# Lightning attention in windows of 256 tokens, on four 64x64 tensor tiles at a time, ahead of an MLP

## The chip, the cores and the metric

The kernel runs on one core of one Trainium2 chip. The metric is the device time of one execution in microseconds (us); less is better. "The span" is the length of the execution that was profiled, which is about 1.7 us shorter than the timed figure of the same execution. Executions carry a state, fast or slow; only fast ones are compared below, unless a sentence says otherwise. A time given alone is the median of all executions of a kernel.

In the views, PE is the engine of matmuls and PEld its weight loads; DVE, ACT and POOL are the vector, scalar and GpSimd engines, SP issues most transfers; PSUM is the memory that PE writes to.

## The reference, cut to what matters

Four batches, eight heads, 768 tokens, head dimension 64. Attention is linear, with a decay `lam` per head, so it runs along the tokens with a 64 x 64 state per head and batch. Its output goes through a mean-centred, scaled MLP of 512 to 2048 to 512 with a residual.

```python
for b in range(nb):                                   # nb blocks along the tokens
    qb, kb, vb = (q[:, :, sl], k[:, :, sl], v[:, :, sl])
    intra = np.einsum('bhic,bhjc->bhij', qb, kb) * Dmask[None]
    intra = np.einsum('bhij,bhjd->bhid', intra, vb)
    inter = np.einsum('bhid,bhde->bhie', qb * lam_pow[None], kv_state)
    out[:, :, sl] = intra + inter
    # ... kv_state = lam_block * kv_state + (decayed k)^T v
# x = out as [batch, token, 512]
xn = (x - mu) / np.sqrt(var + 1e-06) * g_ln
ch = np.maximum(xn @ w_ch1, 0.0) @ w_ch2
return (x + ch).astype(np.float32)
```

## The kernel before

It goes through 24 chunks of 128 tokens, batch after batch. Tokens lie on the 128 partitions, so a load moves 256 B per token and head (64 numbers of 4 B). Attention of a chunk is in steps: casting and scaling (`in_k`, `in_q`, `in_v`), transposes (`p1`), scores and mask, the next state, and the output with the mean and the centred copy (`p3`); `p4` transposes that copy for the MLP. The first projection is `m1`, the second `m2`.

```python
def load_tile(t, after_pool=False):
    b, c = divmod(t, nb)
    # ...
    for name, src in (("k", k), ("q", q), ("v", v)):
        f = inp.tile([128, H, D], F32, tag=name + "in", name=name + "in")
        # ... with after_pool, a POOL write to f delays the load
        nc.sync.dma_start(f, src[b, :, c * C:(c + 1) * C, :].rearrange("h p d -> p h d"))

def scores(t):
    # ...
    for p in range(NP):                # NP = 4 pairs of heads
        for e in range(2):             # two row tiles, 64 rows by 128 columns
            half = slice(e * D, (e + 1) * D)
            nc.tensor.matmul(sc[e][:, p, :], lhsT=s["kT"][half, p, :], rhs=s["qT"][half, p, :], ...)

def next_state(t):
    # ...
    for p in range(NP):                # full array; two of the four 64x64 blocks are not used
        nc.tensor.matmul(pk[:, p, :], lhsT=s["kb"][:, 2 * p:2 * p + 2, :], rhs=s["vb"][:, 2 * p:2 * p + 2, :], ...)

def p3(t):
    # ...
    for h in range(H):
        nc.tensor.matmul(po[:, h, :], lhsT=s["mA"][:, h % 2, h // 2, :], rhs=s["vb"][:, h, :], ...)
    if inter:
        for p in range(NP):
            nc.tensor.matmul(po[:, 2 * p:2 * p + 2, :], lhsT=s["qT"][:, p, :], rhs=s["S"][:, p, :], ...)

# the start, weights and loads only
load_tile(0); load_tile(1); ...; load_tile(2); load_tile(3)
# ... chunk 0 and chunk 1 ...
in_k(2, nc.scalar); in_q(2); load_w1(0); in_v(2)
# ...
in_k(3, nc.scalar); in_q(3); in_v(3); load_w1(1)
# ...
load_w1(2); load_w1(3)
# ... then load_w2(0..3), load_tile(5..7), and MLP groups 0 and 1
```

After the start, a plan of MLP units (one unit is 4 `m2` matmuls, or `m1` work of about the same length, some 0.9 us) has the attention steps put in between by hand.

## Time and profile before

| | before |
|---|---|
| median of the first 3 runs, us | 228.71 (227.81 to 229.04) |
| span, us | 226.0 |
| PE busy | 206.9 us, 92% |
| `m2` starts at, us | 43.9 |
| matmuls | 1736 |

The prediction below shows the page, the chain and the windows. The list of waits of PE before the change (the columns: who waited, for whom, us in total, times, longest):

```profile
PE tk L161 <- DVE kb L141: 5.7, 1, 5.7
PE sc L185 <- ACT qT L172: 2.8, 4, 0.8
...
PE pm L279 <- DMA w<-in_moe_w_ch_dram: 1.6, 1, 1.6
```

The long waits all belong to the start; 5.7 us is the wait for the very first data. No input load stands in the list. The list of DMA issues (how many, KB each, median us from issue to landing):

```profile
vin<-in_v_dram SPq DMA_DIRECT2D x24, 256.0 KB, 4.9
...
w<-in_moe_w_ch_dram POOLq DMA_DIRECT2D x8, 512.0 KB, 8.3
```

### The profile page before, as it was taken

How to read it: one execution, taken by the hardware profiler on the slowest of the kernel's cores; microseconds unless marked ns; L12 is line 12 of the kernel's file. 1: busy time of each engine (PE TensorE's matmuls, PEld its weight loads, DVE VectorE, ACT ScalarE, POOL GpSimd, SP SyncE). 2: the span in 40 equal slices, each digit the busy share in tenths (PEclk: the TensorE clock that was granted, in tenths of full speed). 3: DMA queues.
4: the chain of work that ended last, by engine and by line, in shares of the span. 5: the costliest groups of instructions: out<-in, count | busy, mean ns of one | idle time of the engine just before them, and what ended most of it. 6: DMA issues, size and time to landing. Idle time of an engine off the chain costs nothing.

```text
span 226.0 us, 4339 instructions
## 1 busy us (share of the span) xinstructions
PE 206.9 (92%) x1736; PEld 131.4 (58%) x1736; DVE 104.5 (46%) x202; ACT 95.5 (42%) x191; POOL 88.0 (39%) x103
## 2 busy tenths in 40 slices
PE   0567969999999899999999999999999999999992
PEld 0346848844677587577587466545654565455540
DVE  2467610054457556766754474267428345420021
ACT  5655645611256255146146067404750375127400
POOL 2559518025670948874156638301562020000000
PEclk9999988999999999999999999999999999999999
DMA  5998992999999999999999999939432511040012
GB/s 117 225 228 134 184 211 36 187 191 230 209 290 225 234 239 209 188 226 191 219 200 263 228 219 198 220 100 217 109 70 70 142 25 23 33 131 2 0 67 72
DMA packets 107555, 35.93 MB, mean 159 GB/s; under 512 B 100112, under 2 KB 104464, under 8 KB 107536
## 3 DMA queue, kind: packets, MB, share of 16 engines
q1 hardware_dynamic: 103168, 31.47, 68.8%
q0 software_dynamic: 4224, 4.19, 11.7%
q8 instruction: 13, 0.21, 0.4%
q14 instruction: 6, 0.05, 0.1%
q10 hardware_dynamic: 144, 0.00, 0.0%
HBM read 27.53 MB, written 6.29 MB: 150 GB/s over the span
## 4 chain that ended last, share of the span: by engine, by line
PE 81%; DMA 6%; DVE 4%; SPq 3%; ACT 2%; issue 1%; POOL 1%; DVEq 0%
PE pm L292 36%; PE pm L279 35%; DMA w<-in_moe_w_ch_dram 4%; PE sc L185 3%; SPq L65 3%; DMA qin<-in_q_dram 2%; PE po L224 2%; PE po L228 2%; PE pk L198 1%; DVE stats L233 1%; ACT x L231 1%; DVE xc L237 1%; PE tq L169 1%; DVE Stmp L205 1%; PE xt L255 1%
## 5 line engine op out<-in xcount | busy, mean ns | idle before, releaser
L279 PE MATMUL pm<-xT,w 128*128 128x256 bf16 (+2 forms) x704 | 92.2, 287 | 1.6 <-DMA w<-in_moe_w_ch_dram 1.6
L292 PE MATMUL pm<-w,hT 128*128 128x512 bf16 x384 | 88.2, 379 | 0.0
L282 ACT ACTIVATE hT<-pm 128x384 bf16<-128x384 f32 (+1 forms) x112 | 60.0, 536 | 57.9 <-PE pm L279 57.2
L279 PEld LDWEIGHTS <-w 128*128 128x128 bf16 x704 | 63.6, 100 | 23.9 <-DMA w<-in_moe_w_ch_dram 1.8
L292 PEld LDWEIGHTS <-hT 128*128 128x128 bf16 x384 | 36.2, 98 | 39.2
L206 POOL TENSOR_TENSOR Sn<-Stmp,lamC 128x512 bf16<-128x512 f32 x16 | 20.3, 1271 | 65.4 <-DVE Stmp L205 65.3
L233 DVE BATCH_NORM_STATS2 stats<-x 128x6 f32<-128x512 f32 x24 | 16.7, 694 | 44.4 <-ACT x L231 44.3
L303 DVE SCALAR_TENSOR_TENSOR o<-pm,rstd,x 128x512 f32<-128x512 f32 (+1 forms) x25 | 18.0, 725 | 32.1 <-PE pm L292 31.9
L188 DVE TENSOR_TENSOR mA<-sc,tril 128x512 bf16<-128x512 f32 x48 | 30.7, 682 | 2.8 <-PE sc L185 2.8
L231 ACT COPY x<-po 128x512 f32<-128x512 f32 x24 | 14.0, 584 | 34.9 <-PE po L228 22.7
L149 POOL TENSOR_TENSOR vb<-vin,lam_v 128x512 bf16<-128x512 f32 x24 | 25.1, 1044 | 2.4 <-PE po L224 2.0
L237 DVE SCALAR_TENSOR_TENSOR xc<-po,mv,g_row 128x512 bf16<-128x512 f32 x24 | 18.0, 751 | 2.3
L145 POOL TENSOR_TENSOR kq<-qin,lam_q 128x512 bf16<-128x512 f32 x15 | 15.7, 1044 | 1.2 <-DMA qin<-in_q_dram 1.2
L145 POOL TENSOR_TENSOR qb<-qin,lam_q 128x512 bf16<-128x512 f32 x9 | 9.4, 1042 | 15.3 <-DMA qin<-in_q_dram 14.7
L205 DVE TENSOR_TENSOR Stmp<-pk,Sn 128x512 f32<-128x512 f32 x16 | 10.9, 683 | 4.2 <-PE pk L198 4.1
L224 PEld LDWEIGHTS <-mA 128*128 128x128 bf16 x192 | 9.2, 102 | 3.9 <-DVE mA L188 0.4
L161 PE MATMUL tk<-ident,kb 128*128 128x128 bf16 x36 | 4.4, 259 | 6.8 <-DVE kb L141 5.7
L224 PE MATMUL po<-vb,mA 128*128 128x64 bf16 x192 | 10.4, 199 | 0.1
L141 POOL CAST kq<-kin 128x512 bf16<-128x512 f32 x15 | 9.2, 611 | 2.0 <-DMA kin<-in_k_dram 2.0
L258 ACT ACTIVATE std<-mv,eps_t 128x1 f32<-128x1 f32 x24 | 7.0, 293 | 5.4 <-DVE mv L235 5.4
L163 ACT COPY kT<-tk 128x512 bf16<-128x512 bf16 x9 | 5.2, 581 | 7.9 <-PE tk L161 7.9
L260 DVE RECIPROCAL rstd<-std 128x1 f32<-128x1 f32 x24 | 3.8, 158 | 10.2 <-ACT std L258 10.0
(51 smaller groups left out, 97.3 us busy)
## 6 DMA issues: line engine op xcount, KB each, us to landing
kin<-in_k_dram SPq DMA_DIRECT2D x24, 256.0 KB, 4.5
qin<-in_q_dram SPq DMA_DIRECT2D x24, 256.0 KB, 4.6
vin<-in_v_dram SPq DMA_DIRECT2D x24, 256.0 KB, 4.9
out_dram<-o SPq DMA_DIRECT2D x23, 256.0 KB, 2.9
w<-in_moe_w_ch_dram POOLq DMA_DIRECT2D x8, 512.0 KB, 8.3
g_row<-in_moe_g_ln_dram SPq DMA_DIRECT2D x1, 256.0 KB, 4.6
xT<-xc SPq DMA_TRANSPOSE x16, 3.5
out_dram<-o SPq DMA_DIRECT2D x2, 128.0 KB, 1.8
```

Of the source, the lines that this page charges most:

```text
L145: nc.gpsimd.tensor_tensor(st[t]["qb"], qkv_in[t]["q"], lam_q[:, :, None].to_broadcast([128, H, D]), op=ALU.mult)
L149: nc.gpsimd.tensor_tensor(vb, qkv_in.pop(t)["v"], lam_v[:, :, None].to_broadcast([128, H, D]), op=ALU.mult)
L188: nc.vector.tensor_tensor(mA[:, e], sc[e], tril[:, None, :].to_broadcast([128, NP, 128]), op=ALU.mult)
L206: s["pool"] = lambda: nc.gpsimd.tensor_tensor(Sn, tmp, lamC, op=ALU.mult)
L224: nc.tensor.matmul(po[:, h, :], lhsT=s["mA"][:, h % 2, h // 2, :], rhs=s["vb"][:, h, :], start=(h == 0), stop=(not inter and h == H - 1), ...
L231: nc.scalar.copy(x, po.rearrange("p h d -> p (h d)"))
L233: nc.vector.bn_stats(stats, x)
L237: nc.vector.scalar_tensor_tensor(xc, in0=po.rearrange("p h d -> p (h d)"), scalar=mv[:, 0:1], in1=g_row, op0=ALU.subtract, op1=ALU.mult)
L279: nc.tensor.matmul(pm[:, b, :], lhsT=w1[n // W2K][:, kk, (n % W2K) * 128:(n % W2K + 1) * 128], rhs=xT_of[g][:, kk, 0:N], start=(b == 0 and ...
L282: nc.scalar.activation(hT[:, u * NB:(u + 1) * NB, 0:N], pm, ACT.Relu)
L292: nc.tensor.matmul(acc[i], lhsT=hT[:, kk, i * 128:(i + 1) * 128], rhs=w2[kk // W2K][:, kk % W2K, :], start=(kk == 0), stop=(kk == KB - 1))
L303: nc.vector.scalar_tensor_tensor(o[:, sl], in0=a[:, sl], scalar=rstd, in1=x[:, sl], op0=ALU.mult, op1=ALU.add)
```

## The change

Two chunks of one batch are taken together as a window of 256 tokens; the four batches take turns, so a window's state is needed only four windows later. Chunk a lies on partitions 0 to 63 and chunk b on 64 to 127, two neighbouring tokens on each partition. So a load moves 512 B at once, and each attention matmul uses a 64 x 64 quarter of the PE array, with four different quarters next to each other in the program. No block of a matmul is wasted any more. The price is more matmuls (2848), a row order that the store has to undo (two stores with strided rows), and a short DVE read of the output (`reader`) between the two halves of the state matmuls. The order of the start and the plan are new too.

```diff
-    def load_tile(t, after_pool=False):
-        b, c = divmod(t, nb)
... (cut)
-            nc.sync.dma_start(f, src[b, :, c * C:(c + 1) * C, :].rearrange("h p d -> p h d"))
+    def source(src, u, hs):
+        cc, b = divmod(u, B)
+        return src[b, hs, cc * W:(cc + 1) * W, :].rearrange("h (p j) d -> p h (j d)", j=2)
... (cut)
+    def scores(u, hf, early=False):
... (cut)
+        for i in range(2):
+            for jk in range(2):
+                for ab in range(2):
+                    for e in range(2):
+                        nc.tensor.matmul(sc[e][half[ab], i, jk, :], lhsT=kT[half[e], 2 * hf + i, jk, half[ab]],
+                                         rhs=qT[half[e], 2 * hf + i, :, half[ab]],
... (cut; kv and inter are tiled in the same way)
+    def av(u, pairs, chunks=(0, 1)):
... (cut)
+        for p in pairs:
             for e in range(2):
... (cut)
+                for j in range(2):
+                    for jq in range(2):
+                        for ab in chunks:
+                            nc.tensor.matmul(s["po"][ab][half[jq], 2 * p + e, :],
+                                             lhsT=s[f"mA{p // 2}"][half[ab], e, p % 2, j, half[jq]],
+                                             rhs=s["vb"][half[ab], 2 * p + e, j],
... (cut)
+    def reader(u):
+        s = st[u]
+        for ab in range(2):
+            if s["S"][ab] is not None:
+                seen = wk.tile([128, H], F32, tag="seen", name="seen")
+                nc.vector.tensor_copy(seen, s["po"][ab][:, :, 0])
... (cut)
-    sizes = [2, 2, 1, 1, 2, 2, 2, 3, 3, 3, 3]
+                    nc.sync.dma_start(rows[j][:, ab, sl], o[half[j], ab, sl])
... (cut)
+    sizes = [2, 2, 2, 2, 2, 2, 4, 4, 4]
... (cut; the start, weights and loads only)
+    load_w1(0)
+    load_window(1, after_pool=True)
... (cut)
+    load_w1(1)
+    load_w1(2)
... (cut)
+    in_q(1, nc.gpsimd)
+    in_v(1, nc.gpsimd)
+    load_w1(3)
+    load_window(2, after_pool=True)
+    load_w2(0)
... (cut; the steady part: what is sent ahead of window u)
+    def ahead_of(u):
+
+        for f, w in ((transpose_dma, u + 1), (load_window, u + 3), (p0, u + 2)):
+            if w < NU:
+                f(w)
```

`p0` is the casting and scaling of one window's k, q and v, most of it on POOL. `kv` is the product for the next state, `av` scores times v, `inter` q times state. Tiles in the views: `kq` and `vb` scaled k, q and v; `kqT` the transpose of `kq`; `sc` scores, `mA` the same masked; `pk` state product, `Stmp` its sum with the old state, `Sn` the decayed new state; `po` output, `xc` its centred copy, `xT` the transpose of that; `pm` a product of the MLP.

## The prediction

Its sum: 226.0 - 2.4 - 2.2 - 5.6 - 0.8 = 215.0 us of span, 217.5 us timed. The -2.4 is the choice of 17.6 us for attention, between the cases of 15.6 and 31.2 that stand there.

> **What bounds the kernel now.** I read the page first: the busy line and the forty slices.
>
> ```profile
> span 226.0 us, 4339 instructions
> PE 206.9 (92%) x1736; PEld 131.4 (58%) x1736; DVE 104.5 (46%) x202; ACT 95.5 (42%) x191; POOL 88.0 (39%) x103
> ...
> PE   0567969999999899999999999999999999999992
> ...
> PEclk9999988999999999999999999999999999999999
> DMA  5998992999999999999999999939432511040012
> ```
>
> PE is full from slice 7 (about 40 us) to the end; no other engine passes half. DMA is also full for two thirds of the span, so the second question is whether PE ever waits for it. The chain that ended last, in order of time, answers:
>
> ```profile
> 8.90 5.43 DMA qin<-in_q_dram
> ...
> 22.71 8.51 DMA w<-in_moe_w_ch_dram
> 31.27 10.57 PE pm L279 x80
> 42.29 1.75 PE pm L279 x16
> 44.04 0.86 PE pm L292 x4
> 45.13 0.33 PE sc L185 x8
> ...
> 95.37 0.23 PE po L224 x8
> 95.61 0.22 PE po L228 x4
> ```
>
> Up to 31 us the chain is transfers and a latency chain. From there it is PE, almost without a break: MLP work with small attention pieces between. The first projection's weights land at 31.27, the second projection (L292) starts at 44.04. The table of windows confirms the two stages (columns: stretch, length, then busy time and instructions of PE, PEld, DVE, ACT, POOL, clock, DMA share, GB/s):
>
> ```profile
> 0.00:10.00 10.00, 2.33 (x22) 1.70 (x23) 2.40 (x9) 5.91 (x10) 3.31 (x11) 1.00 0.86 161
> 20.00:30.00 10.00, 8.35 (x86) 6.81 (x83) 6.79 (x14) 6.33 (x14) 5.43 (x7) 1.00 0.98 154
> 30.00:40.00 10.00, 8.73 (x65) 7.21 (x66) 0.17 (x1) 4.68 (x9) 5.69 (x8) 0.83 0.66 112
> 100.00:120.00 20.00, 20.00 (x193) 14.55 (x192) 12.05 (x25) 9.09 (x18) 8.15 (x9) 1.00 1.28 216
> ```
>
> Busy PE is not useful PE, so I took the start-to-start distances of single matmuls in the trace: 216 ns for 512 columns, 56 for 128, 29 for 64 (columns divided by 2.4 plus 2.5 ns). Charging each matmul that much gives **192.3 us of work**. The other 33.7 us of the span: 5.7 before the first matmul, 13.2 in stops over 130 ns (11.6 of them before 31 us), 10.3 in small delays (cold clock before 40 us, and switches below), 4.5 after the last matmul. At 44.04 us, 20.9 us of work is done, so 23 us are lost by then.
>
> [...] the 8 score matmuls (64 rows) start in pairs 3 ns apart, a pair each 56 ns. Four tiles do not occur before. [...] 152 ns from the last full-array matmul to the first score one, 149 ns back, in place of 56, so about 95 ns a switch. [...] In the packet records a 256 B packet takes a median 18 ns, a 2048 B packet 84: a line through both gives 8.6 ns plus 1 ns per 27 B, so I estimate 27.5 ns at 512 B. [...]
>
> **Part by part.**
>
> *MLP matmuls.* Group sizes go from [2,2,1,1,2,2,2,3,3,3,3] to six of 2 and three of 4. m1 before: 320 x 109 + 256 x 162.5 + 128 x 56 = 83.7 us; after: 352 x 109 + 64 x 56 + 192 x 216 = 83.5. m2 stays 384 x 216 = 82.9. No gain.
>
> *Attention matmuls, before.* 192 scores as 96 pairs x 56 = 5.4; 192 po x 29 = 5.6; 80 pk and 80 state matmuls x 56 = 9.0. Sum 20.0 us. Transposes: 104 x 56 = 5.8. With the MLP this is 192.4, which matches the 192.3 counted.
>
> *Attention matmuls, after.* Scores 12 windows x 32 = 384 of 128 columns. Of 64 columns: kv 8 x 32 + 4 x 16 = 320, av 768, inter 8 x 32 + 4 x 16 = 320, so 1408. The loops put four different tiles next to each other. If four run together: 96 quads x 56 = 5.4, 352 quads x 29 = 10.2, sum **15.6 us (-4.4)**. [...] If only two run together: 192 x 56 + 704 x 29 = 31.2 (+11). I choose 17.6 us (-2.4), near the first, because row pairs already behave ideally.
>
> *Transposes.* 48 for k and q (was 72), 16 for the MLP input (was 32): 64 x 56 = 3.6, **-2.2 us**.
>
> *Mode switches.* Before, two per chunk: 24 x 2 x 95 ns = 4.6 us. After, a window's attention runs in two blocks (two switches each): 12 x 4 x 95 ns, the same.
>
> *Loads.* 18.9 MB as 256 B packets: 73728 x 18 / 16 = 83 us of all DMA engines; after, 36864 x 27.5 / 16 = 63, so 20 us of DMA time freed. After 44 us PE waits for no load, so there this is hidden. In the start it counts. Before the m1 weights, the old kernel moves four tiles (3.1 MB) and has issued the first weight load only at 15.4 us; the new one issues it once the first half of k is seen (about 5 us) and loads one window (1.6 MB) ahead of it. My count: window 0 in 5.3 us of DMA, gain vector 0.7, window 1 5.3, four m1 weight chunks at 3.1 each (2 KB read per packet of 96 ns): 23.7 us, plus 2.6 us until the first packet. POOL issues the last m1 chunk only after window 1's v has been scaled (about 20 us), so I put its landing at 27 to 29 us against 31.3. After that about 10.5 us of PE work (the last quarter of group 0, group 1, window 2's scores) precede m2, which then starts at about **39 us instead of 44**. By then 21.5 us of work is done, so 17.5 us are lost instead of 23.1: **-5.6 us**.
>
> *Vector side.* States are 64 x 64 blocks now: 16 DVE sums of 683 ns become 256 elements, an estimated 415 ns, and 16 POOL decays of 1271 about half. Masks stay 48 x 682. Fence reads add 20 x about 0.15 us. All beside PE: worth nothing directly, but with the k, q tiles transposed by DMA earlier I expect the two DVE-bound breaks at 69 to 78 us (1.3 us of stops) to shrink: -0.8.
>
> *Tail.* The last output half, its store and 4.5 us stay.
>
> **Sum.** 226.0 - 2.4 - 2.2 - 5.6 - 0.8 = 215.0 us of span. The timed median is 2.7 us above the traced span, so **217.5 us**, 5% faster.
>
> **Rivals.** (a) *PE becomes issue- or weight-load-bound.* PE instructions rise from 1736 matmuls to about 1856 + 992 = 2848, and a block holds 128 of them. No stretch of the trace before shows PE fed faster than a pair of instructions per 28 ns for longer than 8 matmuls. If only bursts overlap, attention costs 11 us more on the bound engine, and the start's gain is eaten: 226 to 230. For it: no evidence of sustained feeding[...]. Against: the pairs at 3 ns. (b) *The start does not move.* It may stay a chain of load, cast, transpose, copy, scores, mask, av, norm; a whole window of 256 tokens goes through it at once, and window 1 shares the DMA with the weights. Then m2 starts at 44 again and only PE work is saved: 223. For it: in slice 2 to 6 the DMA is at its limit and the bytes before m1 are about the same (7.6 against 8.1 MB). Against: bigger packets. (c) *PSUM waits.* Two state products now borrow two of four "mm" banks until DVE has read them, and the fence puts a DVE round trip between the two halves of the state matmuls. If each of 9 steady windows costs 0.5 us, 222. Against: the fence has four MLP units in between, DVE is under 50% busy. (d) *Everything overlaps ideally* and the weights land at 26: m2 at 36, attention 15.6: 210.
>
> **Range and chances.** Central 217.5; the start is uncertain by 4 us either way, quads by -2 to +13, so 208 to 227. Faster by over 2% means under 224.1: only (a) in full, or two of (b), (c), prevent it: 0.77. Within 2%: 0.17. Slower than 233.3 needs (a) with new waits: 0.06.
>
> **What would show it.** In the single matmul records of a score block, starts 3 to 4 ns apart in fours and a quad each 56 ns (29 for the small ones) confirm the tiling[...]. In the chain of waits the first L-line of the second projection should start near 39 us, with the weight transfer ending at 27 to 29. The packet records should show 512 B packets near 27 ns, the slices a less full DMA after 60 us. From 60 us on PE should show no stops over 0.3 us; if DVE reads of state products or fences stand before PE in the list of waits, (c) is right. PE clock below 0.9 past 40 us would also break the sum.

## The result

The changed kernel took a median of **255.61 us** (252.99 to 257.11, four runs, one of them slow) against 228.88 us for the kernel before. A ratio here is always the mean time of one kernel's fast runs over the mean of the other's in the same rounds, so it is not quite the ratio of the medians. It is **1.1136** (95% interval 1.104 to 1.1233): 11% slower, where 5% faster was predicted. The output is correct.

The page of the changed kernel, the parts that answer to those in the prediction:

```profile
span 254.0 us, 6453 instructions
...
PE 212.4 (84%) x2829; PEld 123.9 (49%) x2848; DVE 101.7 (40%) x216; ACT 85.0 (33%) x154; POOL 74.2 (29%) x92
...
PE   1664892499999949699978996989999899999991
PEclk9999799579999967799999997999999999999998
DMA  5997799579799989986999999326043110430042
```

PE used to be full from slice 7 on. Now it has holes at slices 6 and 7 (38 to 50 us), and again around slices 14 to 26. The granted clock falls in and behind the holes (5 and 7 in slices 7 and 8, 6 and 7 in 14 to 16). DMA is no emptier for its larger packets: it is still nearly full to slice 24, with dips at 21 to 27 and 48 to 54 us.

I split both spans by the starts of single matmuls, charging each its columns divided by 2.4, plus 2.5 ns (a fit to the 216, 56 and 29 ns that the prediction read for 512, 128 and 64 columns), or its distance to the next start where that is shorter (matmuls that run together). A start later than that by over 130 ns is a "stop"; a smaller delay is "small".

| us | before | after | difference |
|---|---|---|---|
| ahead of the first matmul | 5.7 | 5.5 | -0.2 |
| work of matmuls in the record | 192.3 | 184.8 | -7.5 |
| stops before `m2` starts | 11.6 | 21.4 | +9.8 |
| stops after that | 1.6 | 20.4 | +18.8 |
| small delays | 10.3 | 15.8 | +5.5 |
| behind the last matmul's start | 4.6 | 6.1 | +1.5 |
| span | 226.0 | 254.0 | +28.0 |

One correction: 19 of the 2848 matmuls are missing from the record of after. They are some 4.1 us of work (19 x 216 ns), and the gaps that they leave make up some 5 us of the late stops. So the work is about 189 us and the true late stops are about 15.4.

**The start.** The chain of the changed kernel (start in us, length in us, what) shows where `m2` (L383) waited:

```profile
7.86 16.21 DMA vin<-in_v_dram
24.13 1.90 POOL vb L174
...
26.92 0.37 SPq L75
27.33 18.96 DMA qin<-in_q_dram
46.37 2.06 POOL kq L169 x2
...
55.77 0.32 PE pm L383
```

`m2` was predicted at 39 us; it starts at 55.7. Read upward: window 2's q takes 19 us to land. It was issued at 27 us, because POOL, which works in order, had to scale window 1's v first, and that v took 16 us to land. In each case the load shared the DMA with weight chunks: window 1 with `w1`, window 2 with `w2`. The packet records show how the two share. From 18 to 21 us they hold 429 load packets of 512 B and 419 weight packets, each of which writes 1 KB and reads 2 KB: almost one for one. That is 73 GB/s for the load and 143 GB/s for the weights, counted by what is written. How the DMA engines take turns between them is not shown, but the equal counts have a plain consequence: beside a weight chunk, this load with its small packets got a third of the bytes, and its packets took a median 40 ns against 28 with no weight packet near. The same was so before (435 packets against 430 between 45 and 48 us), but there PE needed no load at that time. The list of issues shows the result for all windows (before: 4.9 and 8.3 us):

```profile
vin<-in_v_dram SPq DMA_DIRECT2D x11, 512.0 KB, 8.0
...
w<-in_moe_w_ch_dram POOLq DMA_DIRECT2D x8, 512.0 KB, 11.3
```

The table of windows (stretch, length, busy time of PE, PEld, DVE, ACT, POOL, clock, DMA share, GB/s) has for the ten microseconds in question, where PE before was busy for all of the 10.00:

```profile
40.00:50.00 10.00, 3.20 (x27) 2.47 (x28) 0.28 (x1) 2.08 (x3) 2.58 (x3) 0.66 0.90 175
```

**The rest.** The list of waits of PE after the change:

```profile
PE tp L183 <- POOL kq L169: 8.3, 4, 6.1
...
PE pm L357 <- DMA xT<-xc: 5.5, 2, 3.2
...
PE pm L357 <- DVE Stmp L239: 2.1, 1, 2.1
PE po L270 <- issue: 1.3, 1, 1.3
```

The first line is the start once more (6.1 us of it is window 2's q). The next three are new kinds, all behind 60 us. For the second, MLP input waits for its transposing transfer, which comes behind loads (in the chain `kin` takes 3.14 us from 145.20, then `xT` 5.97 us from 148.33). For the third, the chain has the story:

```profile
92.99 5.65 DMA qin<-in_q_dram
...
100.77 1.86 POOL vb L174
102.63 0.58 POOL Sn L235
103.23 0.43 DVE Stmp L239
103.71 1.05 PE pm L357 x8
```

A load lands late. POOL scales that window's q and v, then decays the state of the window being computed, which has been waiting behind. DVE's next sum waits for that decay, a PSUM buffer of the MLP stays held by the state product, and PE stops 2.2 us. The load was for two windows later; nothing else needed it yet. (x1 and x3 below show that the late load is not even needed for such a stop: POOL's order is enough.)

The fourth wait has no semaphore behind it. It stands where the trace shows instruction fetch: a queue that the page calls "instruction" (q8) moves packets of 16,384 B, each taking 0.9 to 1.6 us, 22 of them after against 13 before. Three such stops (at 123.2, 128.8 and 144.5 us) cost 2.6 us together.

**The tiling itself** works. One block of attention in the timeline of PE (start, length, line, operation, how many):

```profile
117.24 0.45 PE L229 MATMUL pk<-vb,kq 64*64 64x64 bf16 x32
117.51 0.40 PE L205 MATMUL sc<-kqT 64*64 64x128 bf16 x16
117.74 0.75 PE L270 MATMUL po<-vb,mA 64*64 64x64 bf16 x64
118.31 0.32 PE L283 MATMUL po<-Sn,kqT 64*64 64x64 bf16 x16
```

These are 128 matmuls in 1.33 us, including the way in and out. Within a quad (four matmuls on the four quarters), starts are 3 to 4 ns apart (later in the `po` matmuls about 8, evenly); the next quad follows after 32 ns (64 columns) or 55 ns (128 columns). The prediction took 29 and 56. A change of tiling mode costs 92 to 98 ns each way, as predicted (309 ns from a 512-column matmul to the first of `pk`, where 216 is its own distance; 148 to 149 ns from the last score matmul back to an MLP one, where 56 is its own).

### The profile page after: what moved, and what is told of

It reads as the page before. It is cut to its first block, busy times and chain, and to the rows that moved or that the text cites. A ratio compares the mean times of both kernels' runs of the same rounds, so it can differ in the third digit from the quotient of the medians.

```text
span 254.0 us, 6453 instructions
## 1 busy us (share of the span) xinstructions
PE 212.4 (84%) x2829; PEld 123.9 (49%) x2848; DVE 101.7 (40%) x216; ACT 85.0 (33%) x154; POOL 74.2 (29%) x92
## 4 chain that ended last, share of the span: by engine, by line
PE 54%; DMA 24%; POOL 8%; DVE 5%; SPq 4%; issue 2%; ACT 1%; DVEq 0%; ACTq 0%; POOLq 0%
PE pm L383 26%; PE pm L357 22%; DMA qin<-in_q_dram 10%; DMA vin<-in_v_dram 10%; POOL vb L174 3%; DMA kin<-in_k_dram 3%; POOL kq L169 2%; DMA xT<-xc 2%; SPq L189 2%; SPq L75 2%; PE po L270 2%; DVE stats L307 2%; PE sc L205 2%; POOL Sn L235 1%; DVE xc L309 1%
## 5 line engine op out<-in xcount | busy, mean ns | idle before, releaser
L357 PE MATMUL pm<-xT,w 128*128 128x256 bf16 (+1 forms) x539 | 93.6, 332 | 9.4 <-DMA xT<-xc 5.5
L383 PE MATMUL pm<-w,hT 128*128 128x512 bf16 x370 | 85.3, 380 | 1.1 <-issue 0.5
L360 ACT ACTIVATE hT<-pm 128x512 bf16<-128x512 f32 x92 | 53.6, 597 | 82.0 <-PE pm L357 81.9
L357 PEld LDWEIGHTS <-w 128*128 128x128 bf16 x544 | 55.0, 105 | 42.1 <-DMA xT<-xc 6.4
L383 PEld LDWEIGHTS <-hT 128*128 128x128 bf16 x384 | 36.7, 98 | 42.8 <-issue 0.6
L404 DVE SCALAR_TENSOR_TENSOR o<-pm,rstd,x 128x512 f32<-128x512 f32 (+1 forms) x25 | 18.0, 725 | 48.0 <-PE pm L383 31.2
L215 DVE TENSOR_TENSOR mA<-sc,keep 128x512 bf16<-128x512 f32 x44 | 28.2, 682 | 22.5 <-PE sc L205 22.4
L169 POOL TENSOR_TENSOR kq<-qin,lam_q 128x512 bf16<-128x512 f32 (+1 forms) x24 | 24.0, 1019 | 27.2 <-DMA qin<-in_q_dram 27.1
L235 POOL TENSOR_TENSOR Sn<-Stmp,lam_s 128x256 bf16<-128x256 f32 x16 | 9.8, 612 | 60.0 <-DVE Stmp L239 51.3
L174 POOL TENSOR_TENSOR vb<-vin,lam_v 128x1024 bf16<-128x1024 f32 (+1 forms) x13 | 23.1, 1782 | 7.2 <-DMA vin<-in_v_dram 7.2
L239 DVE TENSOR_TENSOR Stmp<-pk,Sn 128x256 f32<-128x256 f32 x16 | 6.7, 418 | 27.6 <-PE pk L229 20.8
L183 PEld LDWEIGHTS <-kq 128*128 128x128 bf16 x48 | 4.0, 122 | 18.8 <-DVE kq L161 9.4
L270 PE MATMUL po<-vb,mA 64*64 64x64 bf16 x768 | 10.3, 199 | 1.9 <-issue 1.3
L205 PE MATMUL sc<-kqT 64*64 64x128 bf16 x352 | 10.0, 227 | 1.5 <-ACT kqT L184 0.9
L270 PEld LDWEIGHTS <-mA 64*64 64x64 bf16 x768 | 9.0, 110 | 3.5 <-issue 2.6
```

The source lines that it names most:

```text
L169: eng.tensor_tensor(dst[:, :, :, j], src[:, :, :, j], lq[:, :, :, j:j + 1].to_broadcast([128, n, 2, D]), op=ALU.mult)
L174: eng.tensor_tensor(st[u]["vb"][:, hs], qkv_in[u]["v"][:, hs], lam_v[:, hs, :, None].to_broadcast([128, n, 2, D]), op=ALU.mult)
L205: nc.tensor.matmul(sc[e][half[ab], i, jk, :], lhsT=kT[half[e], 2 * hf + i, jk, half[ab]], rhs=qT[half[e], 2 * hf + i, :, half[ab]], start= ...
L215: nc.vector.tensor_tensor(s[f"mA{hf}"][:, e], s[f"sc{hf}"][e], kp[:, None, :, :].to_broadcast([128, 2, 2, 128]), op=ALU.mult)
L235: eng.tensor_tensor(dst, src, lam_s[:, :, None].to_broadcast([128, NP, D]), op=ALU.mult)
L270: nc.tensor.matmul(s["po"][ab][half[jq], 2 * p + e, :], lhsT=s[f"mA{p // 2}"][half[ab], e, p % 2, j, half[jq]], rhs=s["vb"][half[ab], 2 * ...
```

## The experiments

Each kernel ran on the same chip as the kernel before, whose medians were 227.8 to 228.7. Runs of different rounds are on different chips, so a difference in us between them is good to about 1 us; the ratios are safer. The theory after the result was: the tiling is sound, and the time went to loads and their order, in three places. (A) Window 2's load is issued too late, and against `w2`. (B) Later, the loads as a whole press on the transposing transfers. (C) POOL's order couples a late load to the state. Rivals: the array or its instruction supply is too slow for four-way bursts, or the plan's pace asks too much.

### Taking each suspect away: x1_noload, x2_win2early, x3_both, x4_poolorder

**x1_noload** is wrong: from window 3 on it uses old data, so no more loads are made.

```diff
     def load_window(u, after_pool=False, parts=1):
+        if u >= 3:
+            qkv_in[u] = qkv_in[u % 3]
+            return
```

> Wrong result on purpose: windows 3 to 11 are not loaded, they work on the buffers of windows 0 to 2, so nine windows of input (14.2 MB) leave the DMA queue and nothing else changes. Theory L (late input loads cause the slowdown; the tiled matmuls are fine): the stops of the matmul stream after 60 us, about 20 us, nearly vanish, while those before 55 us stay; 254 us of span becomes 234 to 239, timed 235 to 241. Rival T (the four-tile matmuls, their weight loads and mode switches stall PE): stops stay, 250 or more. Rival P (POOL is the bottleneck by its own work and order, not by waiting for loads): 245 to 252.

It took 244.62 us (ratio 1.0722, 1.0655 to 1.0789), 11.0 less than the changed kernel. The direction is right and the size a miss: the stops behind `m2`'s start went from 20.4 to 11.6 us (19 matmuls are missing from either record), and a 3.3 us stop of the kind C stayed without any load. The rival that names POOL's own work and order (245 to 252 us) was missed by only 0.4 us. The start did not move, as it should not.

**x2_win2early** keeps all data and moves one load up, behind window 1's.

```diff
     load_window(1, after_pool=True)
+    load_window(2)
 ... (cut)
     load_w1(3)
-    load_window(2, after_pool=True)
```

> One line moved: the loads of window 2 are issued right behind those of window 1, not behind the last m1 weight chunk. Theory L: in the kernel after the change they run packet for packet against five weight chunks and land at 39 to 49 us, and PE stops 6 us for them at 41; here they land by about 30 us, in a stretch in which the DMA was nearly idle (21 to 27 us). Second projection starts near 48 us, not 56; time 246 to 250. Rival S (the start is held by the weights themselves): the second projection starts no earlier, 254 to 257.

It took 244.17 us (1.0673, 1.0608 to 1.0737), 11.4 less. Its one profile fell in the slow state, so I use it only for the start, where the order of events is plain: `m2` started at 46.2 us in place of 55.7, and window 2 had landed by 30. The stops before `m2` are 12.2 us in place of 21.4, nearly those of the kernel before. This settles A.

**x3_both** is x1 and x2 together, and so also wrong.

> Both edits: window 2 early and windows 3 to 11 not loaded (wrong on purpose). If theory L is all of it, what stays is the matmul work counted in the trace (184.8 us) plus start and tail: 226 to 232. Under rival T it stays above 242.

It took 233.36 us (1.0207, 1.0156 to 1.0259), 22.3 less: the two add up within the noise (11.0 + 11.4), so they are different losses. It missed its range by a little more than 1 us. Its list of waits shows two of the stops that remain:

```profile
PE pk L232 <- POOL vb L177: 3.4, 1, 3.4
PE pm L360 <- DVE Stmp L242: 3.1, 1, 3.1
```

The first is still in the start (window 1's v, at 26 us). The second, at 87.7 us, is of kind C, and there is no load for it to wait for: POOL scales two windows in a row, from 76.6 to 86.6 us, and the decay stands behind both. The chain of x3 has it:

```profile
77.75 2.01 POOL kq L172 x2
79.76 1.86 POOL vb L177
81.62 1.11 POOL kq L164 x2
82.73 2.02 POOL kq L172 x2
84.75 1.86 POOL vb L177
87.69 1.40 PE pm L360 x8
```

So POOL's order and its 5 us of scaling per window make this stop; a late load is not needed.

**x4_poolorder** takes C alone. The scaling for window j+2 moves on POOL from ahead of window j's attention to behind it, so that a decay cannot stand behind the scaling of a later window.

```diff
-        for f, w in ((transpose_dma, u + 1), (load_window, u + 3), (p0, u + 2)):
+        for f, w in ((transpose_dma, u + 1), (load_window, u + 3)):
 ... (cut)
-        after[at] = [(s1_s3, j)]
+        after[at] = [(s1_s3, j)] + ([(p0, j + 2)] if j + 2 < NU else [])
```

> From window 7 on the scaling of the next window is put on POOL behind the two state decays of the current window instead of ahead of them. Theory H (POOL stands in its queue before a load that has not landed, and the state decays that PE needs stand behind it): the stops at 100 to 108, 117 to 124 and 135 to 145 us shrink by 5 us or more, time 247 to 251. Rival (the loads themselves are late, the order only passes it on): within 2 us of 255.6.

It took 253.5 us (1.11, 1.1055 to 1.1144), only 2.1 less: a miss, and with these intervals no gain is shown. The stop on the state sum was gone, but stops on the transposing transfers rose from 5.8 to 7.3 us. Removing C alone exposes B.

### Trying to recover it with all data: y1_pace to z2_fill

**y1_pace** builds on x2. Groups of two chunks throughout, and attention windows 16 MLP units apart, so that the DMA has longer for each.

```diff
-    sizes = [2, 2, 2, 2, 2, 2, 4, 4, 4]
+    sizes = [2] * 12
 ... (cut)
-    for at, j, rest in ((40, 5, 4), (56, 6, 4), (65, 7, 4), (73, 8, 4), (89, 9, 4), (105, 10, 4), (121, 11, 4)):
+    for at, j, rest in ((40, 5, 4), (56, 6, 4), (72, 7, 4), (88, 8, 4), (104, 9, 4), (120, 10, 4), (136, 11, 4)):
```

> Window 2 early as before, and the rounds of attention spread evenly: MLP groups of two tiles throughout (one window each), windows 7 to 11 at steps of 16 MLP units instead of 8 to 16, with all loads done. Theory L, second half: after 60 us the loads, transposes and stores of a window take about 10 us of all DMA engines, while the old plan asked for windows 6 to 8 every 9 units (about 10 us with attention), so PE caught up with the loads; at 16 units it should not. The stops after 60 us fall from about 20 to 5 us, time 228 to 233 (from 244.2). Rival G (the stops come from the coarse 256-token pieces: two norms in a row on DVE before PE can go on): over 238.

It took 241.4 us (1.0526, 1.0446 to 1.0607), a clear miss: 2.8 us less than x2, not 11 or more. Stops on transposing transfers stayed at 5.4 us and the state sum at 3.2. So it is not chiefly the plan's mean pace that makes the loads late.

**y2_start** (on y1) issues two weight chunks later, behind window 1's q, so that window 1's v comes sooner.

```diff
-    load_w1(1)
-    load_w1(2)
     open_window(1)
     in_k(1, nc.scalar)
     norm(0, 0, early=True)
     in_q(1, nc.gpsimd)
+    load_w1(1)
+    load_w1(2)
```

> As the run beside it, and two weight chunks are issued behind the scaling of window 1's q instead of ahead of it. Theory S1 (queues share packet for packet, [...] window 1's v lands at 24 to 25 us only for that): v lands at 19 to 21 us, dense PE work begins 3 to 5 us earlier, time 3 to 5 us under the run beside it. Rival (the weights themselves are then late): no gain.

It took 243.2 us (1.0641, 1.0575 to 1.0707): no gain. Window 1's v landed at 19.9 us, early as intended, but `w1`'s second chunk then landed at 27.6 us, and PE waited for that instead:

```profile
PE pm L357 <- DMA w<-in_moe_w_ch_dram: 3.3, 1, 3.3
```

The DMA share in this start is 0.99 or more in each 4 us from 4 to 48: it is bound by the DMA, and a change of order just passes the wait on.

**y3_loadfirst** (on y2) issues each load ahead of the k/q transposing transfer, not behind it:

```diff
-        for f, w in ((transpose_dma, u + 1), (load_window, u + 3), (p0, u + 2)):
+        for f, w in ((load_window, u + 3), (transpose_dma, u + 1), (p0, u + 2)):
```

> As the one before, with each window's loads issued ahead of the transposes of the window in front, which wait for POOL. If the in-order issue queue is still a cause of late loads: 1 to 3 us faster. If pacing has cured it: within 1 us.

It took 241.05 us (1.0545, 1.049 to 1.06), 2.1 less than y2, as expected. Order within the DMA queue seems to matter, by a little (the two intervals just overlap).

**z1_xTfirst** (on y1) sends the k/q transposing transfer of the next window behind the MLP-input transposes, which PE needs sooner.

```diff
-        after[at + rest] = [(s2_s4, j), (p4, j - 1)]
+        after[at + rest] = [(s2_s4, j), (p4, j - 1)] + ([(transpose_dma, j + 1)] if j + 1 < NU else [])
```

> As the paced run, with the transposes of the next window's k and q put behind the transposes of the MLP input in the in-order issue queue, and the loads ahead of both. Theory Q (MLP input transposes that PE is about to need stand in that queue behind transposes that wait for POOL, which waits for a load): the stops put down to the MLP input transposes, 5.4 us in the paced run, fall below 2 us; 236 to 238 us against 241.4. Rival (the DMA engines are simply full there): no change.

It took 238.98 us (1.0489, 1.0436 to 1.0542), just outside the expected range. The medians differ by 2.4 us, but y1's holds a slow execution; the means of fast ones differ by 1.3 us and the intervals overlap, so a gain is not shown. Stops on the MLP-input transposes fell from 5.4 to 3.4 us, and the one on the state sum rose from 3.2 to 4.2.

**z2_fill** (on z1) moves two MLP units of the start (16 matmuls) up, to where PE waited for window 1's v.

```diff
+    rstd_of(0)
+    m1s(m1a, 1)
     kv(1, "po")
     new_state(1, 0, nc.gpsimd)
     st[1]["tmp"] = state_sum(1, 1)
-    rstd_of(0)
-    m1s(m1a, 1)
```

> As the run before it, and the second quarter of the first MLP group is put ahead of window 1's state product, which waits 3.3 us for the scaled v of window 1. If weights are there by then (they land at 21 us): 2 to 3 us less. If PE then waits as long for the next thing: under 1 us.

It took 236.1 us (1.0355, 1.0313 to 1.0397), 2.9 less than z1: a hit.

### Two further tries that failed: z3_xb4, z5_jit

**z3_xb4** (on z2) takes load off the DMA by transposing window 3's k and q, and the MLP input of windows 2 and 3, on PE.

```diff
-    XB = 3
+    XB = 4
 ... (cut)
-        if u >= 2:
+        if u >= 4:
 ... (cut; transpose_pe of window 3 at units 20 and 22)
```

> As the run before it, with window 3's k and q and the MLP input of windows 2 and 3 transposed on PE, as the kernel before the change does for these tokens. Takes 1 MB of 256 B packets off the DMA engines while they are full, adds 32 transposes of 56 ns (1.8 us) to PE. Theory D (full DMA engines hold windows 5 to 7): 2 to 4 us less. Rival: 1 to 3 us more.

It took 242.21 us (1.0596, 1.0543 to 1.0648), 5.8 more than z2 (means of fast executions): a miss. PE waited 4.8 us for the centred copy, in its own order, where a transfer could wait without stopping PE; and three stops beside instruction fetches came to 3.8 us.

**z5_jit** (on y1, with z2's swap) puts everything of the next window as late as it can go: scaling of j+1 behind window j, loads two ahead, k/q transposes last.

```diff
-        after[at] = [(s1_s3, j)]
+        after[at] = [(s1_s3, j)] + ([(p0, j + 1)] if j + 1 < NU else [])
 ... (cut)
+        after[at + rest] += [(load_window, j + 2)] if j + 2 < NU else []
+        after[at + rest] += [(transpose_dma, j + 1)] if j + 1 < NU else []
```

> As the run with the filled start, with loads, scaling and transposes of the windows from 6 on one round later, behind the MLP-input transposes of the round. Theory B (a backlog of loads, issued a full window earlier than needed, delays the transposes that PE waits for): the stop of 3.5 us for the MLP input and that of 3.1 for the state sum both go; 228 to 231. Rival (the loads then come too late): PE waits for scaled k or v instead, 236 and up.

It took 262.34 us (1.1531, 1.146 to 1.1602), a miss by over 30 us and slower than the change itself:

```profile
PE sc L205 <- DMA kqT<-kq: 20.2, 6, 4.5
```

The k/q transposes came too late for the scores. The slack that I took to be unneeded was needed.

### The array and its instructions: y4_av_twice, x5_noload_av2

**y4_av_twice** (on y2) issues each of `av`'s matmuls twice for windows 3 to 11 (the result stays correct), to measure what four-way bursts cost.

```diff
-        for p in pairs:
+        for p in [p for _ in range(2 if u >= 3 else 1) for p in pairs]:
```

> The paced and reordered kernel with the 64 probability-times-value matmuls of windows 3 to 11 done twice, the result the same: 576 more small matmuls on four tiles. The trace says a quad takes 32 ns: 144 x 32 ns = 4.6 us more. [...]

It took 262.13 us (1.1419, 1.1323 to 1.1515), 18 more than y2 (means of fast executions), where the array's own pace asks 4.6 (9 windows x 64 x 8 ns). Its profile fell in the slow state; in it seven stops of 1.8 to 4.2 us, 20.0 us together, wait for no semaphore, each beside an instruction fetch. Was it the full DMA that delayed the fetches?

**x5_noload_av2** repeats the doubling on x3, where the loads are gone (wrong).

> Wrong on purpose: windows 3 to 11 not loaded and window 2 early, as in an earlier run (233.4 us), with the probability-times-value matmuls of windows 3 to 11 done twice. In the loaded kernel the doubling cost about 20 us, in stops without any wait, each beside a fetch of 16 KB of instructions. Theory I1 (the fetches are slow because the DMA engines are full of loads): here the doubling costs the array time and little else, 4 to 7 us, so 238 to 240. Theory I2 [...]: 12 us or more, 246 and up.

(Theory I2: the burst itself uses up instructions faster than they are fetched.)

It took 249.28 us (1.0919, 1.086 to 1.0978), 15.9 more than x3. By the split of the spans, 5.0 us of that is the doubled work itself and 10.8 us is late stops. So a loaded DMA is not what is needed for this loss; the burst alone does it. The timeline of PE in that run (in brackets, the idle time before and what ended it):

```profile
118.87 1.43 PE L273 MATMUL po<-vb,mA 64*64 64x64 bf16 x125
122.83 0.26 PE L273 MATMUL po<-vb,mA 64*64 64x64 bf16 x3 [2.52 <-issue]
```

The packet records show one fetch of 16 KB, from 119.7 to 121.4 us, within this. 125 matmuls, each a weight load and a multiplication, are 250 instructions. How many instructions one fetch brings is not in the trace; the counts give an estimate. x5 makes 27 such fetches, and its 3424 matmuls with their weight loads are 6848 instructions, 254 to a fetch (253 in z4_again, 259 in the changed kernel, 267 before). PE went through the block at 117.24 us above, 128 matmuls and their weight loads, in 1.33 us, while one fetch takes 0.9 to 1.7 us and PE goes on some 1.4 us behind its end here. It does so each time: the twelve such stops of x5 and y4 (0.5 us or more, without gaps that missing records leave) and the three of the changed kernel end 1.3 to 1.6 us behind the end of a fetch. That fetching is the mechanism is inferred from this coincidence; no run changed the fetching itself. In the changed kernel, with half as long a burst, these stops are the 2.6 us given above; in x1, without later loads, a single one of 0.7 us is left, so a loaded DMA may still add to them.

### How far reordering goes: z4_order, z4_again, x6_noload_order

**z4_order** is z2 with x4's edit of POOL's order.

> As the run with the filled start (236.1 us), with the scaling of a coming window behind the two state decays in POOL's order from round 5 on. Theory H (POOL's order): the stop put down to the state sum, 3.1 us, goes; 232 to 234. Rival (the loads behind it are as late): 235 to 237, the stop moves to another name.

Three of its four executions took 231.5 to 233.3 us (ratio of the fast runs 1.0202, 1.015 to 1.0255): a hit, and the best correct form of the change. The fourth, the profiled one, took 528.99 us, with most 512-column matmuls starting 621 ns apart in place of 216; I have no explanation and use nothing of it.

**z4_again** is the same kernel with more rounds.

> The same kernel as z4_order: 232 to 234 us again; in its profile no stop of 3 us put down to the state sum near 89 us (theory H). If that stop is there, the 3 us came from elsewhere.

The long execution did not come back: 234.04 us (232.2 to 234.66, six runs; 1.0211, 1.0166 to 1.0256). All its 3040 matmuls are in the record, which gives a clean figure for the work: 189.2 us. Of the stops behind `m2`'s start, the one on the state sum is gone, and one large one is left:

```profile
PE pm L357 <- DMA xT<-xc: 4.5, 2, 4.3
```

**x6_noload_order** is z4 with x1's edit (wrong): the reordered kernel without loads behind window 2.

> Wrong on purpose: the reordered kernel with windows 3 to 11 not loaded. Nothing presses on the DMA engines or POOL's order any more. If the tiled matmul work of about 187 us counts in full: start and lead 18, small delays 11, tail 6, other stops 3: 225, timed 227, no more than the kernel before. If 232 or more: another cost of the tiled kernel is still hidden.

It took 227.86 us, ratio **1.000** (0.9967 to 1.0032) to the kernel before, as expected. Its wait for the same transfer is nearly gone:

```profile
PE pm L360 <- DMA xT<-xc: 0.5, 1, 0.5
```

The four spans, split as above (the work of after and of x6 lacks the unrecorded matmuls, about 4 and 3 us, which are in their late stops):

| us | before | after | z4_again | x6_noload_order |
|---|---|---|---|---|
| ahead of the first matmul | 5.7 | 5.5 | 5.5 | 5.5 |
| work in the record | 192.3 | 184.8 | 189.2 | 186.1 |
| stops before `m2` | 11.6 | 21.4 | 12.9 | 12.1 |
| stops after | 1.6 | 20.4 | 8.3 | 7.2 |
| small delays | 10.3 | 15.8 | 10.4 | 9.3 |
| behind the last matmul's start | 4.6 | 6.1 | 6.1 | 5.7 |
| span | 226.0 | 254.0 | 232.4 | 225.9 |

So the tiled form only ties even without the loads: the 3 us of work that it saves go into late stops and a longer tail. With the loads, 4.7 us more come on top (232.53, the median of z4_order's fast executions, against 227.86, same chip).

### A lesson for the kernel before: b1_weights

The start of the kernel before ends with the weights. This is the kernel before with the four `w1` chunks issued at the first two places, not spread over three.

```diff
     load_w1(0)
+    load_w1(1)
 ... (cut)
-    load_w1(1)
+    load_w1(2)
+    load_w1(3)
 ... (cut)
-    load_w1(2)
-    load_w1(3)
```

> The kernel before the change with its four m1 weight chunks issued in two steps, each one step earlier. Its DMA engines are half idle from 21 to 24 us, and the last chunk lands at 34.6 us; PE gets dense at 31. Expected: dense 2 to 3 us earlier, 225 to 227 against 228.2. Rival: the chunks then run packet for packet against tiles 2 and 3 of the input and PE waits for those: 229 to 232.

It took 226.49 us (0.9948, 0.9908 to 0.9987), within what was expected, and `m2` started at 41.9 us, 2 sooner. It is a small gain, half a per cent (the interval lies below 1, well within the 2% that still counts as the same), but it beats both kernels with a correct result.

## Why the prediction was wrong

The direction was wrong and the range missed by 28.6 us. Step by step (two slips of its sums have no weight: its `m1` after is 83.4 and not 83.5, and of the 2.7 us from span to timed median only 1.7 are of one and the same execution; the traced one was a fast one):

**Tiling (-2.4) and transposes (-2.2): right in mechanism, a little large.** Quads run together at 32 and 55 ns. z4_again's full record has 189.2 us of work against 192.3: -3.1 where -4.6 was said. (That form has all groups of two chunks; the sum's own figures give its `m1` 83.8 us, as good as the same.) The transposes gave the -2.2, the attention matmuls -1.1 (20.3 to 19.2) and not -2.4: a quad takes 32 ns, not 29, and the loops do not put four tiles together everywhere. `kv` of the last four windows and `inter` of the first four run in pairs, 55 to 71 ns per four matmuls. Of rival (a), nothing showed in the distance of matmuls: the small ones go at 32 ns a quad.

**Mode switches: right**, 92 to 98 ns (95 said).

**Loads, the step that failed, in two sentences.** The first is "m2 starts at about 39 us instead of 44", worth -5.6. It counted the bytes of window 0, window 1 and `w1`, as if each got the DMA in turn, and left out window 2, which the order of the program puts between `w1` and `m2` for PE. Loads and weights shared the DMA packet for packet (429 to 419), so window 1's v came at 24.1 us and held POOL (it was scaled at 26.0 us, where "about 20" was said); window 2 was issued at 27 and shared with `w2`. The weights were not what `m2` waited for: the last `w1` chunk landed at 31.6 us (27 to 29 was said), and before at 34.6, for the 31.27 that the prediction read off the chain is the third chunk. `m2` started at 55.7. The term was +9.8 us of stops in place of -5.6. x2 shows the cause: one moved line gave 11.4 us back. y2 shows that the rest of the hoped-for gain was not there, since the DMA is then full all through the start: rival (b), in full. Without window 2's delay, 44 was about as good as it got (43.2 in z4_again).

The second is "After 44 us PE waits for no load, so there this is hidden". That was read from the kernel before and carried over to a kernel with another order. In it a load is twice as large and comes in bursts, the k/q transposes and the MLP-input transposes queue behind it, and POOL's in-order work ties the state to the scaling of later windows. The result was about 15 us of real late stops where 0.8 us less than before was predicted. Taking the loads away (x1) took 8.8 us of late stops with it, 11.0 us of the time, and x3 shows that this adds to the start's loss. x4 and z4 show C: the state sum's stop vanished when scaling went behind the decay. But C is only in part a matter of loads: it stayed, at 3.3 us, in x1 and x3.

**Packet size: right, but no DMA time was freed.** The 512 B packets, when no weight packet is near, take 28 ns (27.5 was estimated). But the packets of all transfers together took 181.9 us of the 16 engines before and 182.2 after. Loads and transposes (256 and 512 B) fell only from 132.3 to 125.4 us, as more transposes go by DMA (28672 packets, 23552 before), and the stores' 2 KB packets rose from 18.1 to 23.4. So the predicted 20 us were not there to be used. And the wait was one of order and of shares: beside weight packets the 512 B load moved about one packet for each of theirs (429 to 419 from 18 to 21 us).

**Vector side (-0.8): wrong in sign.** Its single figures held: a state sum took 418 ns (an estimated 415), a decay 612 (half of 1271), a fence read 156. DVE and POOL became less busy (DVE 104.5 to 101.7, POOL 88.0 to 74.2 us), yet PE now waits for them. That is rival (c) in another guise: a PSUM buffer held by the state product, but by way of POOL's order and not by the fence, which never showed.

**Instruction supply was not in the sum.** Rival (a) named "PE becomes issue-bound", but looked for it in the distance of matmuls. It came as rare long stops, 2.6 us in the changed kernel by its trace, and some 11 us when the burst was doubled (x5).

**Tail.** It grew by 1.5 us where none was expected. The final store is now split into twice as many; that this is the cause is argued only.

**Small delays.** They grew by 5.5 us. Of the 15.8 us, 7.5 lie in stretches where the record gives half the clock (43.2 to 53.5, 91.0 to 97.8, 104.7 to 108.1 and 155.9 to 159.3 us, in or behind the stops), against 1.6 before. The prediction named this as a sign that its sum is broken. z4_again has 10.4 and x6 9.3, so the growth goes with the stops; that they cause it is inferred.

**What stays open.** z4_order is 4.7 us over its form without loads. One stop of 4.3 us on a transposing transfer (in z4_again) is most of it; y1, y3, z1 and z5 moved such stops about and did not remove them, and z3 put others in their place. The 529 us execution is unexplained. Whether a shorter instruction stream would help could not be separated from the tiling that needs it.

## What to carry to other kernels

That a wait isn't there before is no proof that it won't be there after: when a change alters the size or the order of loads, write down for each load when it is issued, what shares the DMA with it, and which in-order engine stands behind it, before taking it as hidden. Count shares per packet as well as per byte: 429 load packets went with 419 weight packets here, and that was 73 GB/s against 143. And when an array is cut into smaller tiles, count instructions as well as columns: here 128 small matmuls and their weight loads were gone in 1.33 us, and a fetch took 0.9 to 1.7.
